# One token group's second dense product as seven block products, with its sums in the activation buffer and the output weights loaded in row order

## The chip, the cores and the metric

The kernel runs on one core of one Trainium2 chip. The metric is the device time of one execution in microseconds (us). Lower is better. Five engines work in parallel, each on a queue of its own, in order: PE (TensorE, matrix products out of SBUF into PSUM), DVE (VectorE), ACT (ScalarE), POOL (GpSimd) and SP (SyncE, which issues nearly all DMAs). They wait for one another by semaphores.

## The reference

Two layers follow each other. The first is a linear attention with decay, for 4 batches, 8 heads, 768 positions and 64 channels a head; a matrix `kv_state` per head is carried from block to block:

```python
Dmask = np.where(rel >= 0, lam[:, None, None] ** rel[None, :, :], 0.0)
for b in range(nb):                    # 12 blocks of 64 positions
    intra = np.einsum('bhic,bhjc->bhij', qb, kb) * Dmask[None]
    intra = np.einsum('bhij,bhjd->bhid', intra, vb)
    inter = np.einsum('bhid,bhde->bhie', qb * lam_pow[None], kv_state)
    out[:, :, sl] = intra + inter
    kb_dec = kb * rev_pow[None]
    kv_state = lam_block * kv_state + np.einsum('bhsd,bhse->bhde', kb_dec, vb)
```

Its result, 4 x 768 = 3072 tokens of 512 channels, goes through a two-layer network of 2048 hidden units:

```python
h = x @ w_in                           # (3072, 512) @ (512, 2048)
g = 0.5 * h * (1.0 + np.tanh(c * (h + 0.044715 * h * h * h)))
return g @ w_out                       # (3072, 2048) @ (2048, 512), float32
```

Everything comes in and goes out as float32; on the chip the products are made in float16 with float32 sums.

## The kernel before, in words

**Two streams of work, one order.** The attention is cut into 24 steps: a step is 256 positions of one batch and half of the heads, so steps 0 and 1 make the first 256 tokens, 2 and 3 the next. The network is cut into seven groups of tokens, `groups = [[0, 1], [2], [3], [4, 5], [6, 7], [8, 9], [10, 11]]`, in units of 256 tokens: group 0 and groups 3 to 6 have 512 tokens, groups 1 and 2 have 256. A group can begin when its steps are done. `queue_group` (L544) cuts a group into small pieces and appends them to the list `filler`; `fill(n)` takes the next n pieces off it. The main sequence (from L922) is a list written out by hand: steps of the attention and `fill` calls in turn. Every instruction is pinned to the program's order (`pin`), so each engine's queue holds its instructions just as the main sequence gives them. Nothing is reordered: where an engine waits for an operand, all that stands behind waits too.

**One attention step.** `load_step` (L60) issues the loads of q, k and v on SP. `cast_q` (L277) multiplies q by its decay on DVE, `cast_k` (L290) makes k float16 (ACT; for step 4 DVE), `scale_v` (L264) multiplies v by its decay on POOL. `prep` makes the three. Four buffers are held for each of the loaded q, k, v, so the load of step s + 4 waits for the use of step s. `stage_t` (L309) transposes q and k on PE into one PSUM tile `Tps` and copies it out (`qkT`); from step 8 on a transposing DMA does this. `R(n, s)` makes the scores S of step n (L350), the products of step s, and the masked scores PT (L360, DVE, from PSUM). `update` (L491) folds the step into the state `t` (L506, DVE) and multiplies the state by the decay into `u` (L513, POOL), which later products read. `U(n)` is the second half of that.

**One group of the network.** `mm1` (L561) makes a tile of the hidden layer, four matmuls deep, and ACT applies GELU to it into `gT` (L565). `gtp` holds two `gT` buffers, so that one group's second product can run while the next group's first is made. `gT` is 16 chunks of 128 hidden units, by all tokens of the group; HF = 8 chunks are one half.

The second product is made in two ways:

- group 0 densely: `mm2(tau, part)` (L570) multiplies tile tau of 128 tokens (0 to 3) by four chunks of hidden units, four matmuls of 128x512 into one bank of PSUM. 4 tiles x 4 parts = 16 pieces, 64 matmuls. A finished tile is copied by ACT into `o32` and sent by `store_pair` (L539), two tiles at a time, from two places in the main sequence;
- groups 1 to 6 by seven products of half size (the Strassen-Winograd scheme). The 2048 hidden units and the 512 outputs and the tokens are halved, so `gT` and `w_out` are each four blocks. `sum_g` (L602) makes four sums of blocks of `gT` on DVE (L610), `sum_wout` (L122) four sums of blocks of `w_out` (L133, DVE), once for all groups, into `w_sum16`. `product(m, p, part)` (L616) then makes product m of 1 to 7 for token tile p, as matmuls of 256 columns (L640): eight, or four where `part` says which half of the hidden units. Results are put together from banks X (a running sum of products 1, 6, 7, 4, read out on the way), W (2) and Y (5, then 3 on top of it), with copies on ACT (L657) and three additions (DVE twice, POOL once, L692). `FACTORS` gives for each product which block or sum of `gT` meets which block or sum of `w_out`: products 1 and 2 need plain blocks, 5 needs sum 1 of both, 6 sum 2, 3 sum 4 of `gT`, 7 sum 3 of both, and 4 sum 4 of `w_out`. Groups 5 and 6 (`SEVEN`) have their first product in seven blocks as well.

The sums of `gT` need a place. `gs_tiles` (L522) gives groups 1 and 2 the staging buffers of the weights, `w0` and `w1`, that are idle by then.

**Output weights.** `load_wout(j)` (L96) loads rows 512 j to 512 j + 511 of `w_out`, 1 MB, into a staging buffer; the order is j = 0, 2, 1, 3. `cast_wout(j, eng)` (L112) makes them float16, in two halves on two engines: j = 0 both on POOL, 2 both on ACT, 1 and 3 one on POOL and one on ACT. A sum `sum_wout(0, m)` needs blocks 0 and 2, `sum_wout(1, m)` blocks 1 and 3.

**The order before.** In the main sequence (L977 to L1013) stand, in this order: 8 pieces (the last of group 0's hidden layer), the casts of `w_out`, five of the eight weight sums, 9 pieces of the dense product, `prep(4)`, `stage_t(4)`, and then steps 5 to 7, each with its `prep`, `R`, `U`, two pieces, and now and then a weight sum. The last piece of the dense product stands just after `U(6)`; behind it begins the hidden layer of group 1.

Of the kernel before, what the change touches and what calls it, by code (L numbers as in the profile page):

```python
# [15 lines left out]
def kernel(  # L16
# [79 lines left out]
    def load_wout(j):  # L96
        t = wst.tile([P, 4, DM], FP32, tag=f"w{(0, 2, 1, 3)[j]}", name=f"wo32_{j}")
        pin(nc.sync.dma_start(out=t[:], in_=moe_w_out[j * 512 : (j + 1) * 512, :].rearrange(
            "(c p) e -> p c e", p=P)))
        wstage[("o", j)] = t  # L100
# [11 lines left out]
    def cast_wout(j, eng):  # L112
        t = wstage[("o", j)]
        for i in range(2):
            dst = w_out16[:, 4 * j + 2 * i : 4 * j + 2 * i + 2, :]
            src = t[:, 2 * i : 2 * i + 2, :]
            if eng[i] is nc.scalar:
                pin(nc.scalar.activation(out=dst, in_=src, func=AF.Copy))
            else:
                pin(nc.gpsimd.tensor_copy(out=dst, in_=src))  # L120
# [44 lines left out]
    for j in (0, 2, 1, 3):  # L165
        load_wout(j)
# [78 lines left out]
    def prep(s):  # L245
        prep_qk(s)
        prep_v(s)
# [42 lines left out]
    def cast_k(s):  # L290
        tk, k32 = a16[s][1], ld32[s][1]
        if s == 4:
            pin(nc.vector.tensor_copy(out=wide(tk), in_=k32[:]))
        else:
            pin(nc.scalar.activation(out=wide(tk), in_=k32[:], func=AF.Copy))  # L295
# [226 lines left out]
    def gs_tiles(g):  # L522
        if g < 3:
# [13 lines left out]
    o_pairs = {}  # L537

    def store_pair(pair):  # L539
        rows = out[2 * pair * P : 2 * pair * P + 2 * P, :].rearrange("(i p) d -> p i d", p=P)  # L540
        for i in range(2):
            pin(nc.sync.dma_start(out=rows[:, i], in_=o_pairs[pair][:, i]))

    def queue_group(g, lead=0, per_set=0):  # L544
# [23 lines left out]
        O2 = {}  # L568

        def mm2(tau, part):  # L570

            if not O2.get(tau):
                O2[tau] = [ps_M.tile([P, DM], FP32, tag="M", name="O2ps"), 0]
            for f in range(4 * part, 4 * part + 4):
                n = O2[tau][1]
                pin(nc.tensor.matmul(O2[tau][0][:], gT[:, f % HF, f // HF, tau * P : (tau + 1) * P],  # L576
                                     w_out16[:, f, :], start=(n == 0), stop=(n == NF - 1)))
                O2[tau][1] += 1
            if O2[tau][1] < NF:
                return  # L580
            pair = tau // 2
            if pair not in o_pairs:
                o_pairs[pair] = otp.tile([P, 2, DM], FP32, tag="o32", name="o32")
            pin(nc.scalar.activation(out=o_pairs[pair][:, tau % 2], in_=O2.pop(tau)[0][:],
                                     func=AF.Copy))

# [27 lines left out]
        def product(m, p, part=None):  # L616
# [42 lines left out]
            def store(T, ps=slice(0, NP), es=slice(0, 2)):  # L659
# [8 lines left out]
                if g == 2:  # L668
                    kept_stores.append(send)
                else:  # L670
                    send()
# [166 lines left out]
        if g == 0:  # L838
# [9 lines left out]
            order = [(tau, part) for part in (0, 2, 1, 3) for tau in range(3)]  # L848
            order += [(3, part) for part in (0, 2, 1, 3)]
            for tau, part in order:  # L850
                filler.append(lambda tau=tau, part=part: mm2(tau, part))
# [127 lines left out]
    fill(8)  # L979
    cast_wout(2, (ACT, ACT))  # L980
    cast_wout(1, (POOL, ACT))
    cast_wout(3, (POOL, ACT))
    for m in W_SUMS:
        sum_wout(0, m, DVE)
    sum_wout(1, 1, DVE)
    fill(9)
    prep(4)
    stage_t(4)
    prep(5)
    sum_wout(1, 2, DVE)  # L990
    fill(2)
# [3 lines left out]
    prep(6)  # L995
    fill(2)
# [4 lines left out]
    sum_wout(1, 3, DVE)  # L1001
# [3 lines left out]
    fill(1)  # L1005
# [3 lines left out]
    sum_wout(1, 4, DVE)  # L1009
    fill(2)  # L1010
    R(7, 6, lambda: prep_qk(9))
    store_pair(0)
# [5 lines left out]
    for n, (a, b, c, d) in FILL.items():  # L1018
# [11 lines left out]
        if n == 9:  # L1030
            store_pair(1)
# [121 lines left out]
```

## Time and profile before

| what | value |
| --- | --- |
| median of 3 runs | 199.15 us (198.92 to 199.36) |
| span of the profiled execution | 197.1 us |
| time of the shown runs beyond that span | 2.05 us |
| busy share of PE, PE's weight loads, DVE, ACT, POOL | 97%, 71%, 77%, 62%, 37% |
| granted clock of PE | 9 tenths or more in every slice of 40 |
| dense second product of group 0 on PE (L576) | from 31.23 to 49.28, with attention steps in between |
| mean DMA rate over the span | 193 GB/s (38.13 MB in both directions) |

The profile is that of one execution, 197.1 us from first to last instruction; a run's time is what the device counts around it, so the two are compared by their difference. The page cuts the span in 40 slices of 4.93 us and gives for each engine its busy tenths (9 is 90% or more). Rows by line give the tile written, the tile read, shapes, how often, and the mean length of one. In the chain of waits, each step leads back from the last instruction to what released it. Lines of the order of time give start, length, engine, line, operation, tiles, and in brackets the idle time before the instruction, with what ended it.

### The profile page before, as it was taken

How to read it: one execution, taken by the hardware profiler on the slowest of the kernel's cores; microseconds unless marked ns; L12 is line 12 of the kernel's file. 1: busy time of each engine (PE TensorE's matmuls, PEld its weight loads, DVE VectorE, ACT ScalarE, POOL GpSimd, SP SyncE). 2: the span in 40 equal slices, each digit the busy share in tenths (PEclk: the TensorE clock that was granted, in tenths of full speed). 3: DMA queues.
4: the chain of work that ended last, by engine and by line, in shares of the span. 5: the costliest groups of instructions: out<-in, count | busy, mean ns of one | idle time of the engine just before them, and what ended most of it. 6: DMA issues, size and time to landing. Idle time of an engine off the chain costs nothing.

```text
span 197.1 us, 5915 instructions
## 1 busy us (share of the span) xinstructions
PE 191.5 (97%) x2431; PEld 140.0 (71%) x2431; DVE 151.6 (77%) x297; ACT 122.2 (62%) x249; POOL 73.3 (37%) x85
## 2 busy tenths in 40 slices
PE   8979999999999999999999999999999999999993
PEld 2556544446888888654688764588888888888882
DVE  4797622789999889849999937998668996588620
ACT  3673878357874685686835378844768845779221
POOL 6594123456554841068854517165002030002000
PEclk9999999999999999999999999999999999999999
DMA  6999999999999999999997998400220300030205
GB/s 172 290 324 384 387 387 388 299 287 292 236 216 225 259 343 220 213 266 247 271 268 149 268 328 213 88 4 0 53 85 25 109 6 0 0 110 0 106 19 197
DMA packets 62810, 38.13 MB, mean 193 GB/s; under 512 B 18624, under 2 KB 55744, under 8 KB 62784
## 3 DMA queue, kind: packets, MB, share of 16 engines
q1 hardware_dynamic: 62240, 37.50, 75.0%
q8 instruction: 19, 0.31, 0.6%
q10 hardware_dynamic: 544, 0.26, 0.5%
q14 instruction: 7, 0.06, 0.1%
HBM read 27.26 MB, written 6.29 MB: 170 GB/s over the span
## 4 chain that ended last, share of the span: by engine, by line
PE 89%; SPq 4%; DMA 4%; ACT 0%; issue 0%
PE Hps L561 25%; PE MX L640 18%; PE MY L640 9%; PE HX L739 7%; PE O2ps L576 7%; PE MW L640 4%; DMA wi<-in_moe_w_in_dram 4%; SPq L70 4%; PE HY L739 4%; PE S L350 3%; PE Hps L830 3%; PE HW L739 2%; PE OK L408 2%; PE O L461 1%; PE O L436 1%; PE OK L399 1%
## 5 line engine op out<-in xcount | busy, mean ns | idle before, releaser
L561 PE MATMUL Hps<-xT,w_in 128*128 128x512 f16 (+1 forms) x288 | 50.5, 332 | 0.0
L513 POOL TENSOR_TENSOR u<-t,lumask 128x256 f16<-128x256 f32 x40 | 30.9, 787 | 39.5 <-DVE t L506 25.8
L561 PEld LDWEIGHTS <-w_in 128*128 128x128 f16 x288 | 27.9, 98 | 19.1
L565 ACT ACTIVATE gT<-Hps 128x512 f16<-128x512 f32 x56 | 33.3, 597 | 11.3 <-PE Hps L561 10.8
L360 DVE TENSOR_TENSOR PT<-S,mask 128x512 f16<-128x512 f32 x48 | 30.3, 681 | 7.5 <-PE S L350 7.5
L266 POOL TENSOR_TENSOR v<-v,dv 128x512 f16<-128x512 f32 x24 | 27.7, 1156 | 18.2 <-DMA v<-in_v_dram 14.2
L640 PEld LDWEIGHTS <-gs 128*128 128x128 f16 x320 | 31.2, 98 | 3.6
L640 PEld LDWEIGHTS <-gT 128*128 128x128 f16 x240 | 23.3, 98 | 3.2 <-ACT gT L565 0.2
L640 PE MATMUL MX<-w_sum,gs 128*128 128x256 f16 x160 | 21.4, 273 | 0.0
L282 DVE TENSOR_TENSOR qk<-q,dq 128x512 f16<-128x512 f32 x23 | 18.4, 802 | 1.7 <-DMA q<-in_q_dram 1.7
L692 POOL TENSOR_TENSOR o<-u,q 128x512 f32<-128x512 f32 (+1 forms) x5 | 6.3, 1253 | 35.2 <-ACT u L657 35.2
L295 ACT ACTIVATE qk<-k 128x512 f16<-128x512 f32 x23 | 14.4, 625 | 7.4 <-DMA k<-in_k_dram 7.2
L610 DVE TENSOR_TENSOR gs<-gT 128x1024 f16<-128x1024 f16 (+1 forms) x24 | 16.9, 711 | 1.6 <-ACT gT L565 1.6
L576 PE MATMUL O2ps<-w_out,gT 128*128 128x512 f16 x64 | 14.6, 379 | 0.0
L487 ACT ACTIVATE xT<-OK 128x256 f16<-128x256 f32 x26 | 9.9, 452 | 6.7 <-PE OK L408 6.2
L739 PEld LDWEIGHTS <-ws 128*128 128x128 f16 x128 | 12.5, 97 | 1.8
L657 ACT ACTIVATE u<-MX 128x256 f32<-128x256 f32 x18 | 6.9, 384 | 10.1 <-PE MX L640 10.1
L487 ACT ACTIVATE xT<-O 128x256 f16<-128x256 f32 x22 | 8.0, 459 | 5.3 <-PE O L461 4.5
L576 PEld LDWEIGHTS <-gT 128*128 128x128 f16 x64 | 6.1, 98 | 6.6
L640 PE MATMUL MY<-w_out,gs 128*128 128x256 f16 x80 | 10.7, 273 | 0.0
L350 PEld LDWEIGHTS <-qkT 64*64 64x64 f16 x384 | 6.0, 106 | 6.6 <-issue 3.6
L640 PE MATMUL MX<-w_sum,gT 128*128 128x256 f16 x80 | 10.4, 273 | 0.0
(96 smaller groups left out, 317.3 us busy)
## 6 DMA issues: line engine op xcount, KB each, us to landing
q<-in_q_dram SPq DMA_DIRECT2D x24, 256.0 KB, 5.1
k<-in_k_dram SPq DMA_DIRECT2D x24, 256.0 KB, 5.1
v<-in_v_dram SPq DMA_DIRECT2D x23, 256.0 KB, 5.4
out_dram<-o SPq DMA_DIRECT2D x23, 256.0 KB, 4.2
wo<-in_moe_w_out_dram SPq DMA_DIRECT2D x4, 1024.0 KB, 9.5
wi<-in_moe_w_in_dram SPq DMA_DIRECT2D x4, 512.0 KB, 8.0
wi<-in_moe_w_in_dram SPq DMA_DIRECT2D x2, 1024.0 KB, 12.7
v<-in_v_dram ACTq DMA_DIRECT2D x1, 256.0 KB, 4.2
```

The costliest lines, as they stand in the source:

```text
L266: pin(nc.gpsimd.tensor_tensor(wide(tv[:]), ld32[s][2][:], decay(dv, s), ALU.mult))
L282: pin(q_eng.tensor_tensor(wide(tq), q32[:], decay(dq, s), ALU.mult))
L295: pin(nc.scalar.activation(out=wide(tk), in_=k32[:], func=AF.Copy))
L360: pin(nc.vector.tensor_tensor(t[:, hl].rearrange("p b c d -> p b (c d)"), Sps[:].rearrange("p b c d -> p b (c d)"), mask[:].unsqueeze(1).t ...
L487: pin(nc.scalar.activation(out=d, in_=o, func=AF.Copy))
L513: pin(nc.gpsimd.tensor_tensor(u[:], state[half][:].unsqueeze(2).to_broadcast([P, 2, 2, D]), lumask[:, 2 * half : 2 * half + 2, :].unsqueez ...
L561: pin(nc.tensor.matmul(by_block(Hps[:, i, :]), w_in16[:, c, f * P : (f + 1) * P], x(c), start=(c == 0), stop=(c == NC - 1)))
L565: pin(nc.scalar.activation(out=dst, in_=Hps[:], func=AF.Gelu_apprx_tanh))
L576: pin(nc.tensor.matmul(O2[tau][0][:], gT[:, f % HF, f // HF, tau * P : (tau + 1) * P], w_out16[:, f, :], start=(n == 0), stop=(n == NF - 1)))
L610: pin(nc.vector.tensor_tensor(g_rows(m, i), g_rows(a, i), g_rows(b, i), op))
L640: pin(nc.tensor.matmul(dst, lhsT, rhs, start=(opens and i == 0), stop=(closes and i == HF - 1), skip_group_check=True))
L739: pin(nc.tensor.matmul(dst[:, i, :], w_in_block(a, slice(c, c + 1), slice(f * P, f * P + P))[:, 0], x_block(b, slice(c, c + 1))[:, 0], sta ...
```

## The change

Group 0's second product goes through `product` as the other groups' does. Its pieces stand in the order (1, 0) (5, 0) (1, 1) (5, 1) (2, 0) (3, 0) (6, 0) (2, 1) (6, 1) (3, 1) (7, 0) (7, 1) (4, 0) (4, 1) of (product, half of the hidden units), each for two token tiles: 28 pieces of four matmuls with 256 columns in place of 16 pieces of four with 512. The `mm2` of before is gone.

The eight sums of `gT` for group 0 are made on DVE, each over four chunks and 256 tokens (128x1024). They are held in a second tile of `gtp`, the buffer that group 1's `gT` takes later.

`w_out` is loaded in the order 0, 1, 2, 3. The first half of blocks 1 to 3 is made float16 on DVE, the second on ACT; block 0 stays on POOL. The k of step 4 is made float16 on ACT. The casts and the sums of weights stand at other places between the pieces. Groups of pieces (`fill`) between the attention steps are larger: 4 instead of 2 ahead of `R(4, None)`, for example. The stores of the two halves of group 0's output are kept (`o_sends`) and issued at the places where `store_pair` stood, one row block of 128 tokens a DMA, as before.

```diff
--- before.py
+++ after.py
@@ -94,7 +94,7 @@
         pin(nc.sync.dma_start(out=t[:, cs, :], in_=src[:, cs, :]))
 
     def load_wout(j):
-        t = wst.tile([P, 4, DM], FP32, tag=f"w{(0, 2, 1, 3)[j]}", name=f"wo32_{j}")
+        t = wst.tile([P, 4, DM], FP32, tag=f"w{j}", name=f"wo32_{j}")
         pin(nc.sync.dma_start(out=t[:], in_=moe_w_out[j * 512 : (j + 1) * 512, :].rearrange(
             "(c p) e -> p c e", p=P)))
         wstage[("o", j)] = t
@@ -117,7 +117,7 @@
             if eng[i] is nc.scalar:
                 pin(nc.scalar.activation(out=dst, in_=src, func=AF.Copy))
             else:
-                pin(nc.gpsimd.tensor_copy(out=dst, in_=src))
+                pin(eng[i].tensor_copy(out=dst, in_=src))
 
     def sum_wout(j, m, eng):
 
@@ -162,7 +162,7 @@
     for j in range(1, 4):
         for part in ((0, 1) if j < 2 else (None,)):
             load_win(j, part)
-    for j in (0, 2, 1, 3):
+    for j in range(4):
         load_wout(j)
     for s in range(4, 9):
         load_step(s)
@@ -289,10 +289,7 @@
 
     def cast_k(s):
         tk, k32 = a16[s][1], ld32[s][1]
-        if s == 4:
-            pin(nc.vector.tensor_copy(out=wide(tk), in_=k32[:]))
-        else:
-            pin(nc.scalar.activation(out=wide(tk), in_=k32[:], func=AF.Copy))
+        pin(nc.scalar.activation(out=wide(tk), in_=k32[:], func=AF.Copy))
 
     whole_qk = {}
 
@@ -520,7 +517,13 @@
     gs_kept = []
 
     def gs_tiles(g):
-        if g < 3:
+        if g == 0:
+            if not gs_kept:
+                t = gtp.tile([P, HF, 2, 2 * SB], FP16, tag="gT", name="gs_0")
+                t = t[:].rearrange("p i f n -> p (i f n)").rearrange(
+                    "p (k i n) -> p k i n", k=4, i=HF)
+                gs_kept[:] = [0, t[:, 0:2], t[:, 2:4]]
+        elif g < 3:
             if not gs_kept or gs_kept[0] != g:
                 gs_kept[:] = [g, wst.tile([P, 4, HF, P], FP16, tag=f"w{g - 1}", name=f"gs_{g}")]
         elif not gs_kept or gs_kept[0] < 3:
@@ -534,12 +537,8 @@
     group_of = {sb: (g, i) for g, sbs in enumerate(groups) for i, sb in enumerate(sbs)}
     filler = []
     kept_stores = []
-    o_pairs = {}
-
-    def store_pair(pair):
-        rows = out[2 * pair * P : 2 * pair * P + 2 * P, :].rearrange("(i p) d -> p i d", p=P)
-        for i in range(2):
-            pin(nc.sync.dma_start(out=rows[:, i], in_=o_pairs[pair][:, i]))
+    o_sends = []
+    sum_of = {}
 
     def queue_group(g, lead=0, per_set=0):
         N = len(groups[g]) * SB
@@ -565,27 +564,6 @@
             pin(nc.scalar.activation(out=dst, in_=Hps[:], func=AF.Gelu_apprx_tanh))
 
         row0 = groups[g][0] * SB
-        O2 = {}
-
-        def mm2(tau, part):
-
-            if not O2.get(tau):
-                O2[tau] = [ps_M.tile([P, DM], FP32, tag="M", name="O2ps"), 0]
-            for f in range(4 * part, 4 * part + 4):
-                n = O2[tau][1]
-                pin(nc.tensor.matmul(O2[tau][0][:], gT[:, f % HF, f // HF, tau * P : (tau + 1) * P],
-                                     w_out16[:, f, :], start=(n == 0), stop=(n == NF - 1)))
-                O2[tau][1] += 1
-            if O2[tau][1] < NF:
-                return
-            pair = tau // 2
-            if pair not in o_pairs:
-                o_pairs[pair] = otp.tile([P, 2, DM], FP32, tag="o32", name="o32")
-            pin(nc.scalar.activation(out=o_pairs[pair][:, tau % 2], in_=O2.pop(tau)[0][:],
-                                     func=AF.Copy))
-
-
-
         HN = N // 2
         G_SUMS = {1: ((1, 0), ALU.add, (1, 1)), 2: (1, ALU.subtract, (0, 0)),
                   3: ((0, 0), ALU.subtract, (1, 0)), 4: ((0, 1), ALU.subtract, 2)}
@@ -665,7 +643,9 @@
                     for i in [slice(i, i + 1) for i in range(ps.start, ps.stop)]:
                         pin(nc.sync.dma_start(out=rows[:, i, es], in_=o[:, i, es, :]))
 
-                if g == 2:
+                if g == 0:
+                    o_sends.append(send)
+                elif g == 2:
                     kept_stores.append(send)
                 else:
                     send()
@@ -845,10 +825,11 @@
                     filler.append(lambda f=f, stage=stage: mm1_part(f, *stage))
             for f in range(8, NF):
                 filler.append(lambda f=f: mm1([f]))
-            order = [(tau, part) for part in (0, 2, 1, 3) for tau in range(3)]
-            order += [(3, part) for part in (0, 2, 1, 3)]
-            for tau, part in order:
-                filler.append(lambda tau=tau, part=part: mm2(tau, part))
+            sum_of[0] = sum_g
+            for m, part in ((1, 0), (5, 0), (1, 1), (5, 1), (2, 0), (3, 0), (6, 0), (2, 1), (6, 1),
+                            (3, 1), (7, 0), (7, 1), (4, 0), (4, 1)):
+                for p in range(HN // P):
+                    filler.append(lambda m=m, p=p, part=part: product(m, p, part))
             return
         def behind(k, i0, i1, ms):
 
@@ -976,40 +957,53 @@
     cast_win(3)
     DVE, ACT, POOL = nc.vector, nc.scalar, nc.gpsimd
     cast_wout(0, (POOL, POOL))
-    fill(8)
-    cast_wout(2, (ACT, ACT))
-    cast_wout(1, (POOL, ACT))
-    cast_wout(3, (POOL, ACT))
-    for m in W_SUMS:
-        sum_wout(0, m, DVE)
+    sum_0 = sum_of[0]
+    fill(4)
+    sum_0(0, 4, (1, 2))
+    sum_wout(0, 1, DVE)
+    sum_0(0, 4, (4,))
+    fill(4)
+    cast_wout(1, (DVE, ACT))
+    sum_0(4, 8, (1,))
     sum_wout(1, 1, DVE)
-    fill(9)
+    sum_0(4, 8, (2, 4))
+    fill(6)
+    cast_wout(2, (DVE, ACT))
+    fill(2)
+    sum_wout(0, 2, DVE)
+    sum_wout(0, 3, DVE)
+    sum_0(0, 4, (3,))
+    fill(6)
+    cast_wout(3, (DVE, ACT))
+    sum_wout(1, 2, DVE)
     prep(4)
+    fill(4)
+    sum_0(4, 8, (3,))
     stage_t(4)
     prep(5)
-    sum_wout(1, 2, DVE)
-    fill(2)
+    sum_wout(1, 3, DVE)
+    fill(4)
     R(4, None)
     stage_t(5)
     U(4)
     prep(6)
+    sum_wout(0, 4, DVE)
     fill(2)
     R(5, 4)
     stage_t(6)
     U(5)
     prep(7)
-    sum_wout(1, 3, DVE)
+    sum_wout(1, 4, DVE)
     fill(2)
     R(6, 5)
     U(6)
-    fill(1)
+    fill(2)
     prep(8)
     fill(1)
     stage_t(7)
-    sum_wout(1, 4, DVE)
     fill(2)
     R(7, 6, lambda: prep_qk(9))
-    store_pair(0)
+    o_sends.pop(0)()
     U(7)
     scale_v(9)
     fill(2)
@@ -1028,7 +1022,7 @@
         if n < 11:
             load_step(n + 4, "qkv" if n < 10 else "qk")
         if n == 9:
-            store_pair(1)
+            o_sends.pop(0)()
         if n == 11:
             scale_v(13)
             load_step(14, "v")
```

## The prediction

> **What bounds the kernel now.** I read the busy rows and slices of the page first, then the chain of waits, then the order of time of DVE and of POOL around the change. The page's rows for the whole span:
>
> ```profile
> PE 191.5 (97%) x2431; PEld 140.0 (71%) x2431; DVE 151.6 (77%) x297; ACT 122.2 (62%) x249; POOL 73.3 (37%) x85
> ...
> PE   8979999999999999999999999999999999999993
> ...
> DVE  4797622789999889849999937998668996588620
> ```
>
> PE is the bound: from slice 4 (20 us) almost to the end it has no idle tenth. DVE has a hole in slices 5 to 8 (25 to 40 us, tenths 6, 2, 2, 7), just ahead of the stage that is changed, and from slice 9 on it is nearly full too. The chain of waits has the changed stage; columns are start, length, what:
>
> ```profile
> 24.32 6.91 PE Hps L561 x32
> 31.23 7.77 PE O2ps L576 x36
> 39.00 0.53 PE Tps L321 x8
> 39.53 1.73 PE O2ps L576 x8
> ...
> 48.42 0.86 PE O2ps L576 x4
> 49.28 0.87 PE Hps L561 x8
> ...
> 59.52 0.87 PE MW L640 x8
> ```
>
> The dense product starts at 31.23 and has its last piece done at 49.28, with no gap between pieces. 8 of its 512-column matmuls take 1.73 us, 0.216 each; 8 of the 256-column matmuls of the seven-block form (L640) take 0.87, 0.109 each. Now DVE and POOL in the same stretch (start, length, instruction, idle before it):
>
> ```profile
> 25.90 1.29 DVE L110 CAST w_in<-wi 128x1024 f16<-128x1024 f32 x2 [1.39 <-DMA wi<-in_moe_w_in_dram]
> 30.63 0.69 DVE L133 TENSOR_TENSOR w_sum<-w_out 128x1024 f16<-128x1024 f16 x1 [3.44 <-POOL w_out L120]
> 33.79 0.69 DVE L133 TENSOR_TENSOR w_sum<-w_out,w_sum 128x1024 f16<-128x1024 f16 x1 [2.46 <-ACT w_out L118]
> 34.40 1.52 DVE L133 TENSOR_TENSOR w_sum<-w_out 128x1024 f16<-128x1024 f16 x1
> ...
> 46.78 1.10 DVE L133 TENSOR_TENSOR w_sum<-w_out 128x1024 f16<-128x1024 f16 x1
> ```
>
> ```profile
> 28.58 2.02 POOL L120 CAST w_out<-wo 128x1024 f16<-128x1024 f32 x2 [6.56 <-DMA wo<-in_moe_w_out_dram]
> 33.99 1.38 POOL L120 CAST w_out<-wo 128x1024 f16<-128x1024 f32 x1 [3.40 <-DMA wo<-in_moe_w_out_dram]
> ...
> 46.43 0.90 POOL L513 TENSOR_TENSOR u<-t,lumask 128x256 f16<-128x256 f32 x1 [0.49 <-DVE t L506]
> 47.55 1.22 POOL L266 TENSOR_TENSOR v<-v,dv 128x512 f16<-128x512 f32 x1 [0.22 <-DMA v<-in_v_dram]
> ```
>
> Two things are to be seen. DVE's hole is some 6 us of waiting for output weights. And DVE and POOL take turns: the sum of 0.69 us at 34.40 took 1.52 and ended 0.55 after POOL's cast (33.99 to 35.37); that cast took 1.38 instead of 1.01 because the sum before it ran to 34.48. Likewise the sum at 46.78 ended 0.55 after POOL's u (47.33), and POOL's v at 47.55 ended 0.90 after that sum (47.88). So where a DVE operation reads two SBUF tensors beside a POOL operation, the second waits for the whole of the first. Operations that read PSUM (L360 at 42.32, 0.68 long beside a v of 1.04) don't show it.
>
> **PE's part.** Out go 64 matmuls, 64 x 0.216 = 13.83 us; in come 7 products x 2 tiles x 8 blocks = 112 of 256 columns, 112 x 0.109 = 12.23. On a PE that never waits that is -1.60 us. Weight loads rise from 64 to 112, 98 ns each by the row of L640, under a matmul of 109: covered, as everywhere in L640. The Trainium skill differs here: "TensorE: Matmul & The Clock Gate", Back-to-back issue gap, gives a sustained 81 ns per matmul at 128 columns and 131 ns at 512, with weight loads in the stream. By a straight line between them 256 columns cost about 98 (my estimate), and the sum would be 112 x 98 ns less 64 x 131 ns, 2.6 us more. The chain above decides for 0.216 and 0.109.
>
> **Where the saving falls.** 18 half products (4 matmuls, 0.437 us each) stand ahead of the transposes of step 4, 7.86 us, against 36 dense matmuls, 7.77. Up to there nothing is saved; the 1.6 us lie in the ten pieces behind.
>
> **What DVE gets.** New: 8 sums of gT (L610 form 128x1024), 3 casts of output weights (128x1024), 2 output sums from PSUM (128x512); gone: the k cast of step 4. Back to back each of the new ones costs 0.605 us (35.84 to 36.44; the two casts at 25.90 take 1.29 with their overlap), so 13 x 0.605 - 0.35 = +7.5 us, more than the hole. The eight sums of the weights stay but move ahead. POOL loses two casts and gets one 128x512 sum, about 1.04 us by the v rows of that shape. ACT loses one weight cast and four copies of O2ps (0.58) and gets nine small copies (0.38 to 0.60) and the k cast: I cost it at nothing, since what PE waits for on it (the halves of blocks 1 to 3 at about 32.8, 35.7 and 37.9, from casts of 1.05 us) is never last below.
>
> **DVE's queue, one by one.** It is in order, so a product that needs one tensor waits for all ahead of it. The weights land as now: blocks 0 to 3 of w_out at 28.5, 31.2, 33.9, 36.8 (the casts that wait for them).
> - Sum 1 of gT (first half) starts when ACT's GELU number 12 ends, 28.45, and runs to 29.13. POOL's first cast, ready at 28.58, then takes its turn to 30.03; sum 2 to 30.57; POOL's second cast to 31.47 instead of 30.60. The first weight sum waits for it: 31.51 to 32.19.
> - From there 13 more, one each 0.605 with 0.05 to 0.1 where one needs the one before: sum 4; cast of block 1 (ends 33.40); sum 1; weight sum 1 of the second half (34.61); sums 2 and 4; cast of block 2 (36.53); weight sums 2 and 3; sum 3; cast of block 3 (39.06); weight sum 2, second half (39.78).
> - PE against this: product 1 is up to 0.1 late, 5 another 0.1, 1b waits for 33.40 (0.3), 5b for 34.61 (0.3), and product 2, ready at 35.53, waits until 36.6 for the cast of block 2: 1.1 us. Then PE runs to 41.0 without a wait.
> - POOL's v of step 4, landed at 39.54, gets the turn at 39.78; the q product of step 4 follows it and ends at 41.26 (now 38.56). The transposes of step 4 start at 41.35 instead of 39.00: **+2.35 us**.
> - Behind it: output sum, sum 3, copy of qkT (43.07), q of step 5 after POOL's v (43.95), weight sum 3 (44.55), output sum, the two masks PT of step 4 (46.36), the state (46.74). Now these masks end at 43.00. POOL's u of step 4 needs the state, takes its turn after the q of step 6 (47.34) and ends at 47.81; PE has been at that product since 46.7: 1.2 us. Queued behind u stand v of step 6 (49.27), the output sum on POOL (50.3) and u of step 5, which also lets q of step 7 ahead: 51.3. PE waits for that u from 50.65, 0.8 us; small waits (0.1 to 0.35) are at 7b, S5 and S6.
> - The last weight sum comes after q of step 7 and that u: 51.87. Product 4b waits for it, and the first layer of group 1 starts at about 52.8 instead of 49.28.
>
> **Sum: +3.5 us**, that is, about 5 us of waits on PE less the 1.6 saved. Behind 49.28 PE is full to the end, so nothing gives it back; DVE is 1.28 us lighter there (its weight sum at 51.25 is done), so I see no new wait.
>
> **Bounds.** Below: without any turn-taking, the same queue with 0.605 a piece gives the cast of block 2 at 35.7, the q of step 4 at 39.5, and the last weight sum at 48.8: +0.4 us. Above: the ledger has no cost for restarting PE after some ten waits; 0.05 to 0.1 each (the weight load of 98 ns) gives +4.3. I take the value with turns, as all five rows of this stretch where the two meet show them.
>
> **What is moved but costs nothing.** SyncE's queue keeps its order and its bytes: four loads of w_out of 1 MB, only rows exchanged, and stores of the same rows at the same places. Its loads of steps 8, 9, 10 wait for the q products of 4, 5, 6: 41.3, 44.0, 47.3 against issues at 42.75, 45.56, 48.62, so 1.3 us of cover; if that goes, each load is late by what is missing. The first transposing DMA (50.66, behind the q product of step 8) moves to about 55, its reader S8 from 58.5 to 62.0, and it lands 6.6 us after issue: still ahead.
>
> The profiled execution spans 197.1 us; the median of the three runs is 199.15, 2.05 more, which I hold constant. So 199.15 + 3.5 = 202.6.
>
> **Rivals.**
> - **The ledger with few collisions.** If the phases fall so that DVE and POOL seldom meet, the lower bound is nearer: +0.4 to +2.2, 199.5 to 201.4. For it: a POOL operation just missed costs nothing, and PE's own waits shift what POOL waits for. Against: DVE has no pause left in which POOL could slip in.
> - **Faster.** DVE keeps up and PE's saving comes through: 199.15 - 1.6 = 197.5. It decides at one place, the cast of block 2 that product 2 waits for: it would have to end before 34.7, when PE gets there, and the last weight sum before 46.8. Eleven operations from 28.45 at 0.605 end at 35.1 even if the wait for POOL were nothing, so DVE would have to be faster per piece than any row of these shapes. Were it so, the transposing DMA for S16 would still cap it: issued at 88.73 and landing 4.4 us later at the earliest, 93.1, while S16 starts at about 93.9; 0.8 us of gain, 198.35.
> - **The same.** DVE's waits and PE's saving cancel within 0.4 us (0.2%, about what a measurement of this kernel can tell from no change).
>
> **Chances.** The full ledger 0.57, with its own range 201.4 to 203.6; few collisions 0.28; faster 0.10; the same 0.05. The range 199.5 to 203.7 leaves out the faster and same cases and a little above. Faster by over 0.2%: 0.10; within: 0.06 (with the edge of the second case); slower: 0.84.
>
> **What would show it.** Right: DVE in slices 6 to 9 at nine tenths, PE with gaps ahead of the W product (the block-2 cast), of the transposes of step 4 and of the products with u; POOL's first two casts ending near 31.5; the first Hps of 128x256 at 52 to 53. Wrong: PE without gaps from 31 to 47, or DVE's sums beside POOL's casts at 0.68. The forecast fails if DVE's pieces are closer than 0.6 us, or if the turns fall otherwise.

## The result and the profile after

The changed kernel took 203.87 us (median of 4 runs, 203.46 to 204.44) beside 199.10 for the kernel before: a ratio of 1.0242 with a 95% interval of 1.0223 to 1.0262, so 4.8 us slower. The forecast was 202.6, with a range of 199.5 to 203.7. The direction was right; the size fell out of the range by 0.17 us. Two disturbed executions of the run without sums are left out below (201.75 and 201.87 stay), and the reordered kernel's profile, with a granted clock of 0.89 from 10 to 16 us and of 0.74 from 16 to 20, begins the changed stage 1.1 us late.

The profiled execution spans 202.7 us and is that of the slowest run (204.44). The rows that answer to those shown of before, first the busy rows of the page:

```profile
PE 190.9 (94%) x2477; PEld 144.2 (71%) x2479; DVE 163.0 (80%) x309; ACT 123.4 (61%) x254; POOL 74.1 (37%) x84
...
PE   8879999897799999999799999999999999999993
...
DVE  4987568999999979879989937999778997588620
```

PE has less work than before (190.9 us against 191.5) in a longer span. Behind slice 2 (slices are counted from 0) its tenths fall below 9 in slices 7, 9 and 10 (35 to 40 us and 46 to 56 us) and once more in slice 19 (96 to 101 us). DVE has lost its hole: slice 6 is at 8, and slices 7 to 13 are at nine tenths or more. The chain of waits (start, length, what) now runs through DVE in the stage that was changed:

```profile
31.43 0.69 DVE w_sum L133
32.12 0.60 DVE gs L588
...
38.46 0.62 DVE w_out L120
39.17 0.69 DVE w_sum L133
39.86 1.45 DVE qk L282
...
51.04 1.03 DVE w_sum L133
52.11 1.03 PE MX L618 x8
53.14 0.87 PE Hps L560 x8
...
63.38 0.87 PE MW L618 x8
...
92.47 6.66 DMA qkT<-qk
99.17 0.42 PE S L347 x16
```

The first hidden layer of group 1 starts at 53.14 instead of 49.28, 3.86 us later. The second place is at the end of the lines: the scores of step 16 hang on a transposing DMA, which was not in the chain before. PE's waits from 28 us on (us in total, times, the longest) name both:

```profile
PE OK L405 <- POOL u L510: 1.6, 2, 0.8
PE S L347 <- DMA qkT<-qk: 1.3, 1, 1.3
PE MW L618 <- DVE w_out L120: 0.9, 1, 0.9
PE S L347 <- ACT qkT L325: 0.6, 2, 0.3
PE Tps L318 <- DVE qk L282: 0.3, 1, 0.3
```

The kernel before has not one line in this view. In the order of time of DVE and of POOL, the turns are where they were expected:

```profile
29.09 1.41 DVE L588 TENSOR_TENSOR gs<-gs,gT 128x1024 f16<-128x1024 f16 x1
31.43 0.69 DVE L133 TENSOR_TENSOR w_sum<-w_out 128x1024 f16<-128x1024 f16 x1 [0.94 <-POOL w_out L120]
...
39.78 1.53 DVE L282 TENSOR_TENSOR qk<-q,dq 128x512 f16<-128x512 f32 x1
```

```profile
28.59 2.80 POOL L120 CAST w_out<-wo 128x1024 f16<-128x1024 f32 x2 [6.66 <-DMA wo<-in_moe_w_out_dram]
39.52 1.24 POOL L266 TENSOR_TENSOR v<-v,dv 128x512 f16<-128x512 f32 x1 [8.13 <-DMA v<-in_v_dram]
```

Sum 2 took 1.41 us beside a cast on POOL, against 0.69 alone. The q product of step 4 took 1.53 behind v. It ended at 41.31, and the transposes of step 4 could not start before that.

To compare runs, the stage is cut in two by three rows of the order of time: the start of group 0's second product, of the transposes of step 4, and of group 1's hidden layer. "Excess" is what is lost behind that: how much later than in the kernel before the hidden-layer pieces behind the scores of step 16 begin (95.37 in its chain), less how much later group 1's hidden layer begins (49.28 there). Times are medians, each taken beside the kernel before at 198.93 to 199.10; the other columns come from one profiled execution each.

| kernel | time, us | product to step 4 | step 4 to group 1 | sum | excess up to step 16 |
| --- | --- | --- | --- | --- | --- |
| before | 199.10 | 7.77 | 10.28 | 18.05 | |
| changed | 203.87 | 10.39 | 11.61 | 22.00 | 1.49 |
| e1, no sums of gT | 201.75, 201.87 | 8.81 | 10.97 | 19.78 | 0.88 |
| e2, casts on ACT | 204.77 | 10.47 | 11.61 | 22.08 | 0.65 |
| e3, block 0 on DVE | 203.26 | 9.25 | 12.09 | 21.34 | 0.65 |
| e4, DMA of step 16 early | 203.44 | 10.37 | 11.62 | 21.99 | 0.17 |
| f1, late weight sums moved too | 202.27 | 8.45 | 9.79 | 18.24 | 2.66 |
| f2, output sum late | 203.31 | 10.39 | 11.11 | 21.50 | 0.37 |
| f4, reordered | 202.05 | 8.48 | 11.63 | 20.11 | 0.00 |
| g1, dense with DVE's work | 201.47 | 10.39 | 10.13 | 20.52 | 0.00 |
| g2, more cover | 204.89 | 10.39 | 11.94 | 22.33 | 1.25 |
| g4, casts on POOL | 204.71 | 10.76 | 11.62 | 22.38 | 0.54 |

### The profile page after: what moved, and what is told of

Same layout as the page of the kernel before. It is cut to its first block, busy times and chain, and to the rows that moved or that the text cites. A ratio compares the mean times of both kernels' runs of the same rounds, so it can differ in the third digit from the quotient of the medians.

```text
span 202.7 us, 6031 instructions
## 1 busy us (share of the span) xinstructions
PE 190.9 (94%) x2477; PEld 144.2 (71%) x2479; DVE 163.0 (80%) x309; ACT 123.4 (61%) x254; POOL 74.1 (37%) x84
## 4 chain that ended last, share of the span: by engine, by line
PE 69%; DMA 12%; DVE 10%; SPq 4%; POOL 1%; issue 1%; ACT 1%; DVEq 0%
PE Hps L560 18%; PE MX L618 18%; PE MY L618 9%; PE HX L719 7%; DMA wo<-in_moe_w_out_dram 5%; PE MW L618 4%; DMA wi<-in_moe_w_in_dram 4%; SPq L70 4%; PE HY L719 4%; DMA qkT<-qk 3%; DVE w_sum L133 3%; PE S L347 3%; DVE qk L282 2%; PE HW L719 2%; DVE gs L588 2%; POOL w_out L120 1%
## 5 line engine op out<-in xcount | busy, mean ns | idle before, releaser
L560 PE MATMUL Hps<-xT,w_in 128*128 128x512 f16 (+1 forms) x288 | 50.5, 332 | 0.0
L618 PEld LDWEIGHTS <-gs 128*128 128x128 f16 x384 | 37.3, 98 | 4.8 <-issue 0.3
L618 PEld LDWEIGHTS <-gT 128*128 128x128 f16 x288 | 27.8, 98 | 6.0 <-DVE w_out L120 1.2
L618 PE MATMUL MX<-w_sum,gs 128*128 128x256 f16 x192 | 25.5, 273 | 0.0
L588 DVE TENSOR_TENSOR gs<-gT 128x1024 f16<-128x1024 f16 (+1 forms) x28 | 20.3, 731 | 3.6 <-ACT gT L564 3.6
L282 DVE TENSOR_TENSOR qk<-q,dq 128x512 f16<-128x512 f32 x23 | 21.5, 937 | 0.0
L618 PE MATMUL MY<-w_out,gs 128*128 128x256 f16 x96 | 12.8, 273 | 0.0
L618 PE MATMUL MX<-w_sum,gT 128*128 128x256 f16 x96 | 12.4, 273 | 0.3 <-DVE w_sum L133 0.3
L618 PE MATMUL MW<-w_out,gT 128*128 128x256 f16 x96 | 11.8, 273 | 0.9 <-DVE w_out L120 0.9
L618 PE MATMUL MY<-w_sum,gs 128*128 128x256 f16 x96 | 12.3, 273 | 0.2 <-DVE w_sum L133 0.2
L618 PE MATMUL MX<-w_out,gT 128*128 128x256 f16 x96 | 12.0, 273 | 0.2 <-DVE w_out L120 0.2
```

The lines of the kernel that those rows point to most:

```text
L282: pin(q_eng.tensor_tensor(wide(tq), q32[:], decay(dq, s), ALU.mult))
L560: pin(nc.tensor.matmul(by_block(Hps[:, i, :]), w_in16[:, c, f * P : (f + 1) * P], x(c), start=(c == 0), stop=(c == NC - 1)))
L588: pin(nc.vector.tensor_tensor(g_rows(m, i), g_rows(a, i), g_rows(b, i), op))
L618: pin(nc.tensor.matmul(dst, lhsT, rhs, start=(opens and i == 0), stop=(closes and i == HF - 1), skip_group_check=True))
```

## The experiments

The theory: VectorE's in-order queue, with its turns against GpSimd, sets the time from 28 to 52 us. Its rivals: the seven-block form costs PE the time by itself; the load order does; the halved cover between the attention steps does (ahead of the scores of steps 5 and 6 still stand two pieces, but a piece is now 0.44 us of PE's work instead of 0.86; only ahead of those of step 4 did the number double); and for the part behind 53 us, the transposing DMA of step 16.

### VectorE's part alone, with the dense product (g1)

```diff
-            for m, part in ((1, 0), (5, 0), (1, 1), ...): ... product(m, p, part)
+            order = [(tau, part) for part in range(4) for tau in range(3)]
+            order += [(3, part) for part in range(4)]
+            for tau, part in order:
+                filler.append(lambda tau=tau, part=part: mm2(tau, part))
...
-    fill(6)
+    fill(3)
```

> The changed kernel with the dense second product of group 0 put back (16 pieces, parts in the order 0 to 3, 9 of them ahead of step 4 and 2, 2, 2, 1 between the steps as before), while VectorE's casts, sums of weights and the eight sums of gT stay where the change put them; the sums of gT are read by nobody. Theory (VectorE's queue sets the time, in whatever form the product is): the q product of step 4 still ends at about 41.2 and its transposes start at about 41.3, 2.3 us later than before; from there PE's 10.28 us of the kernel before give 51.6 to 52.2 for the first hidden layer of group 1, so 2.3 to 2.9 us more, and with 0 to 1 us at the transposing DMA of step 16 the time is 201.4 to 203.0. Rival (the seven-block form itself costs the time, by its waits for sums and its short pieces): no wait ahead of step 4, and within 0.8 us of the kernel before, at most 199.8.

It took 201.47 us, a ratio of 1.0147 (1.0107 to 1.0188). Chain and PE's waits of this kernel:

```profile
39.81 1.46 DVE qk L282
41.32 0.62 PE Tps L318 x8
...
51.61 0.87 PE Hps L566 x8
```

```profile
PE Tps L318 <- DVE qk L282: 2.1, 1, 2.1
PE O2ps L581 <- DVE w_out L120: 0.2, 1, 0.2
```

The dense product waits for no sum, and still the transposes of step 4 start at 41.32, as in the changed kernel, since the q product of step 4 stands behind the same 13 operations from 31.4 us on. That is one wait of 2.1 us in one place, 2.5 us in the time: half of the loss, with PE's form of product taken out, and as the theory had it (201.4 to 203.0; the rival gave at most 199.8). From there to group 1 it needs 10.13 us, no more than before, so the late casts and sums hurt there only where a product waits for them. The changed kernel needs 11.61, although PE's own work is less by 1.68: seven dense pieces (6.05 us) have become ten half pieces (4.37).

### Without the sums of gT (e1), and without the late weight sums too (f1)

```diff
+            if t in G_SUMS and g:
+                return gsum[t][:, i, :]
             if t in G_SUMS:
-                return gsum[t][:, i, :]
+                t = ((1, 0), (0, 0), (0, 1), (1, 1))[t - 1]
...
-            for m in ms:
+            for m in (ms if g else ()):
```

> The changed kernel without the eight sums of gT of group 0: products 5, 6, 3 and 7 read a plain block of gT in place of a sum, so group 0's output is wrong, while PE, ACT, POOL and the loads do the same as before. Theory (VectorE's queue is the bound from 28 to 52 us): eight operations of 0.605 us, 4.8 us, leave it; PE's waits for casts, q and u go, PE keeps its saving of 1.6, and the first hidden layer of group 1 starts at about 47.8 instead of 53.14. Then 197.5 to 198.5, the upper end where the transposing DMA of step 16 comes last. Rival (the smaller matmuls, their restarts or the load order cost PE the time, whatever VectorE does): still above 202.

Both kernels leave out group 0's sums of gT, so its output is not the product. In f1, group 0's products read plain blocks of the output weights as well, and the three late weight sums move:

```diff
-    sum_wout(1, 3, DVE)
     fill(4)
     R(4, None)
...
-    sum_wout(0, 4, DVE)
...
-    sum_wout(1, 4, DVE)
     fill(2)
     R(6, 5)
     U(6)
     fill(2)
+    sum_wout(1, 3, DVE)
+    sum_wout(0, 4, DVE)
+    sum_wout(1, 4, DVE)
     prep(8)
```

> The changed kernel without the sums of gT of group 0, as in the run without sums, and with group 0's products reading plain blocks of the output weights in place of weight sums, so that the three weight sums that stood between attention steps 4 to 7 can be made behind U(6); group 0's output is wrong. Theory (VectorE's own queue sets the pace of steps 4 to 7 even without the sums of gT): the transposes of step 4 start at about 40.0 as without sums, and the stretch from there to the first hidden layer of group 1 shrinks from 10.97 to 8.6 to 9.3 us, so that starts at 48.7 to 49.4; time 198.5 to 200.5, by what the transposing DMA of step 16 adds. Rival (two half pieces of 0.44 us between the attention steps are too short a cover for scores, mask, state and u, whatever else VectorE has to do): the waits for u of 0.8 and for the copies of the transposes stay, and it starts at 50.5 or later.

Both theories missed in e1. Taking 4.8 us off VectorE shortened the stage by 2.2, not by 5.3: 1.6 ahead of step 4 and 0.6 behind. Behind step 4 VectorE is as busy as in the changed kernel, without a gap from 41.19 to 51, because a copy, masks, states, q products, output sums and three weight sums are left. f1 takes the three weight sums out of there, and this part falls to 9.79, the whole stage to 18.24, 0.19 above the kernel before. So the loss of the stage is VectorE's: the sums of gT ahead of step 4, the weight sums behind it. What f1 moved came back at step 7 (order of time of DVE, then of PE, in f1):

```profile
50.44 2.55 DVE L133 TENSOR_TENSOR w_sum<-w_out,w_sum 128x1024 f16<-128x1024 f16 x2
52.91 0.68 DVE L282 TENSOR_TENSOR qk<-q,dq 128x512 f16<-128x512 f32 x1
53.51 0.68 DVE L327 COPY qkT<-Tps 128x1024 f16<-128x1024 f16 x1
```

```profile
54.24 0.42 PE L347 MATMUL S<-qkT 64*64 64x128 f16 x16 [1.61 <-DVE qkT L327]
```

The scores of step 7 wait 1.61 us for a copy behind those sums, and the scores of step 16 wait 0.6 for their transposing DMA. Most of what f1 took above its expectation (202.27 against 198.5 to 200.5) is these two waits: work on a full queue that is pushed back is not gone. f1 also shows a floor. Even where no product waits for a sum, the 1.6 us that PE saves do not appear. Two waits of 0.30 us for copies of the transposes on ACT and one of 0.36 for u stay in the stage, as f1's rival (the short cover) had it, though it starts group 1 well before the rival's 50.5; how much of the floor they make was not isolated.

### Block casts on other engines (e2, e3, g4)

```diff
-    cast_wout(0, (POOL, POOL))
...
+    cast_wout(0, (DVE, DVE))      # e3, between sums 1 and 2 of gT
...
-    cast_wout(1, (DVE, ACT))
+    cast_wout(1, (ACT, ACT))      # e2; 2 and 3 likewise
+    cast_wout(1, (POOL, ACT))     # g4; 2 and 3 likewise
```

> The changed kernel with the first halves of blocks 1 to 3 of the output weights cast on ScalarE too, so VectorE loses three casts of 0.605 us. Theory (VectorE's queue): product 2 no longer waits 0.9 us for the cast of block 2, and everything behind is up to 1.8 us earlier: first hidden layer of group 1 at 51.3 to 51.6, time 201.9 to 202.4. Rival (the weights themselves land too late in row order): the wait ahead of product 2 stays, with another releaser, and the time stays within 0.4 us of 203.9.

> The changed kernel with both casts of block 0 on VectorE, between sums 1 and 2 of gT, instead of on GpSimd. VectorE has 1.2 us more work, and nobody to take turns with from 28 to 39 us. Theory (taking turns costs as much as the work): sum 2 no longer takes 1.41 us, the first weight sum no longer waits 0.94 us for GpSimd; the work from there on is 0 to 0.5 us earlier, time 203.3 to 203.9. Rival (only the amount of VectorE's own work counts): 1.2 us more, 204.8 to 205.2.

> The changed kernel with the first halves of blocks 1 to 3 cast on GpSimd again, as in the kernel before. Theory (GpSimd and VectorE take turns): each cast of about 1.0 us on GpSimd holds VectorE up for that long, against 0.605 for VectorE doing it itself, and product 2 waits no less; 0 to 1.4 us slower than the changed kernel, 203.8 to 205.3. Rival (only VectorE's own work counts): 1.8 us of work leave VectorE, 202.0 to 202.7.

e2 came out at 204.77, outside both ranges. Product 2 still waits about 1.0 us, with another releaser, as the rival had it, but the cause is not late weights. The chain of waits in e2 shows ACT's own order:

```profile
33.89 0.83 PE MX L618 x6
34.74 0.38 ACT m L635
35.13 1.89 ACT w_out L118 x2
37.02 0.49 ACT q L635
37.51 1.90 ACT w_out L118 x2
39.42 0.69 DVE w_sum L133
```

The casts of block 2 stand behind the copy of product 1, which waits for product 1, which waits for the casts of block 1. One full queue was exchanged for another: the last cast ends at 39.41 where VectorE ended it at 39.08. This is why nothing was gained; the profiled execution took 203.93, and what the others (up to 205.28) lost beyond it is not shown.

e3 gave 203.26, 0.04 below the range of the theory of turns and far from its rival's: VectorE does 1.2 us more, and the stretch up to step 4 is 1.14 us shorter. 0.48 of that is given back behind step 4. g4 gave 204.71, as the same theory had it; a weight sum of g4 beside POOL's third cast, from the order of time of DVE and POOL:

```profile
31.34 1.54 DVE L133 TENSOR_TENSOR w_sum<-w_out 128x1024 f16<-128x1024 f16 x1 [0.93 <-POOL w_out L120]
```

```profile
28.59 3.75 POOL L120 CAST w_out<-wo 128x1024 f16<-128x1024 f32 x3 [6.75 <-DMA wo<-in_moe_w_out_dram]
```

The same sum took 0.69 in the changed kernel, where POOL was idle by then. The Trainium skill, "SBUF — State Buffer", section "SBUF: two separate sides", says that an operation of VectorE with two SBUF inputs and one of GpSimd that reads SBUF contend for a shared pair of ports: whichever starts first has it for its whole instruction, and the other is blocked; the 1.54 against 0.69 here and the 1.41 above agree with it.

### Cover between the steps, and GpSimd's output sum (g2, f2)

```diff
     prep(4)
-    fill(4)
...
-    fill(2)      # g2: two of them, ahead of R(5, 4) and of R(6, 5)
+    fill(4)
```

> The changed kernel with four half pieces more between the steps: 14 instead of 18 ahead of the transposes of step 4, then 4, 4, 4 and 2 instead of 4, 2, 2 and 2. Theory (VectorE is busy without a pause from 31.4 to 52 us, so PE only waits elsewhere): VectorE still has no idle time between steps 4 and 7, its last weight sum ends at 51.5 to 52.2, the first hidden layer of group 1 starts at 52.5 to 53.3, time 203.2 to 204.0. Rival (the halved cover between the steps): the waits for u go without others in their place, and it starts 1 us or more earlier, time 202.0 to 202.9.

```diff
-                    pin(nc.gpsimd.tensor_tensor(out_tile(1)[:, :, 1, :], ...))
+                    late.append(add)      # f2: called behind U(6)
```

> The changed kernel with GpSimd's output sum of group 0 (1.27 us, ahead of u of step 5) moved behind U(6). Theory (VectorE is the bound): the wait of 0.81 us for u of step 5 shrinks or goes, but the last weight sum still ends at about 52 us and product 4 waits for it; time 0 to 0.3 us less, 203.5 to 203.9. Rival (GpSimd's queue ahead of u is the bound): 0.8 less, about 203.0.

g2 took 204.89. The waits for u are gone, as the rival had it, and others stand in their place: 2.1 us for the q product of step 4 instead of 0.3, and 1.4 for a copy of product 7 on ACT. Its hidden layer of group 1 starts at 53.67, 0.4 past what either theory gave. The last weight sum ended at 52.02, within the theory's range, and VectorE has no pause above 0.15 us between step 4 and that sum. But the wait of 1.4 is not VectorE's: in g2's chain it hangs on ACT's queue, where copies into xT and qkT and a k cast stand ahead of the copy of product 7. Four half pieces, 1.75 us of PE's work, went behind step 4; the first part stayed at 10.39 and the second grew by 0.33. So cover moved from the one side to the other gains nothing here; that the short cover has no part in the loss is not shown.

f2 took 203.31, between the two expectations. The wait for u of step 5 fell from 0.81 to about 0.3, and the second part is 0.5 us shorter. The theory had missed that the q product of step 7, which took 1.10 behind that u, would then take 0.60 on VectorE itself. So some of VectorE's time is GpSimd's doing.

### The order of loading alone (g3), and a reordered VectorE queue (f4)

```diff
-    for j in (0, 2, 1, 3):
+    for j in range(4):
...
-            order = [(tau, part) for part in (0, 2, 1, 3) for tau in range(3)]
+            order = [(tau, part) for part in range(4) for tau in range(3)]
...
-    cast_wout(2, (ACT, ACT))
-    cast_wout(1, (POOL, ACT))
+    cast_wout(1, (ACT, ACT))
+    cast_wout(2, (POOL, ACT))
```

> The kernel before with only the order of the output weights changed: rows loaded in the order 0, 1, 2, 3, the dense pieces in the same order of parts, casts on ScalarE and GpSimd as before in that order, the weight sums of the second half first. Theory (the load order is no cause): block 2 is float16 at about 35 us and its first dense piece starts at 36.4, so nothing waits, and the time is 198.8 to 199.3. Rival (row order makes PE wait for weights): 0.5 us or more above.

It took 198.94, a ratio of 0.9998 (0.9989 to 1.0008). The load order costs the dense kernel nothing.

```diff
-    cast_wout(0, (POOL, POOL))
...
-    sum_0(0, 4, (1, 2))
+    sum_0(0, 4, (1,))
+    cast_wout(0, (DVE, DVE))
     sum_wout(0, 1, DVE)
-    sum_0(0, 4, (4,))
+    sum_0(0, 4, (2,))
...
-    sum_0(4, 8, (2, 4))
-    fill(6)
+    sum_0(0, 4, (4,))
+    fill(4)
     cast_wout(2, (DVE, ACT))
-    fill(2)
+    sum_0(4, 8, (2,))
     sum_wout(0, 2, DVE)
+    fill(4)
+    sum_0(4, 8, (4,))
     sum_wout(0, 3, DVE)
...
-        elif s in (5, 6, 8):
+        elif s in (4, 5, 6, 8):
```

> The changed kernel with VectorE's queue ordered by when the weights land: casts of block 0 on VectorE, each block's cast and weight sum as soon as it can be, sums of gT in between, the copy of the transposes of step 4 on ScalarE, GpSimd's output sum behind U(6), the transposing DMA of step 16 early. Theory (the loss is VectorE's order and load, not the product form): about 3 us come back; product 2 starts at 35.0 to 35.5 instead of 36.52, the transposes of step 4 at 39.5 to 40.0, the first hidden layer of group 1 at 50.0 to 50.8; time 199.5 to 200.6. Rival (halved cover between the steps): it starts at 51.5 or later, time above 201.3.

The order by landing times, with f2's and e4's edits in it, took 202.05 (200.63 to 202.34). The part up to step 4 fell to 8.48, 1.91 of the 2.62 us back. The part behind stayed at 11.63: the copy of step 4's transposes had left VectorE and GpSimd's output sum had left the way, but one sum of gT had come in, beside v. Without the late start of its profiled execution, the transposes of step 4 stand at 39.5 and group 1 at 51.3, so the expectation held in the first half and not in the second. The time lies above its range (199.5 to 200.6) and on the side of its rival, the halved cover, which gave more than 201.3. No version of the seven-block form that was tried beats the kernel before.

### The transposing DMA of step 16 (e4, f3, h1, h2)

```diff
             load_step(15, "v")
-            load_step(16, "v")
             scale_v(15)
...
     cast_qk(16)
-    load_step(17, "qk")
     transpose_dma(16)
+    load_step(16, "v")
+    load_step(17, "qk")
     load_step(17, "v")
```

> The changed kernel with the transposing DMA of step 16 issued ahead of the loads of v 16, q 17 and k 17 on SyncE instead of behind them. Theory (of the loss of 4.8 us, 3.86 lie ahead of group 1 and the rest in the scores of step 16, which wait for that DMA): the DMA is issued some 1.7 us earlier, the scores of step 16 wait no more, the first hidden layer of group 1 stays at 53.1, and the time falls by 0.6 to 1.2 to about 203.0. Rival (the scores of step 16 are not where the rest goes, and the wait returns at the next transposing DMA): within 0.3 us of 203.9.

> The kernel before with the transposing DMA of step 16 issued ahead of the loads of v 16, q 17 and k 17. Theory: nobody waits for that DMA before the change (it lands 0.8 us ahead of its reader), so the time stays within 0.2 us of the kernel before, 199.0. Rival (the loads pushed back are needed, or the DMA was a hidden wait there too): over 0.4 us either way.

The same edit on both kernels gave 203.44 (from 203.38 to 204.85) and 199.23. In the changed kernel the wait at the scores of step 16 was gone in the profile, the excess 0.17 instead of 1.49, but the median fell by only 0.43, less than expected, and the ratio to the kernel before did not fall at all (1.0244, 1.0205 to 1.0284): e4 alone does not price this wait. On the kernel before the edit changed the time by a factor of 1.0012 (1.0003 to 1.0022), 0.26 us where 0.2 was expected, and not for the better, so nothing waits for this DMA there. To settle it, the DMA was taken out of both kernels:

```diff
-        if s >= FIRST_DMA_T:
+        if s >= FIRST_DMA_T and s != 16:
...
-    fill(5)
+    fill(2)
+    stage_t(16)
+    fill(3)
```

> The changed kernel with step 16 transposed on TensorE, as steps 4 to 7 are, in place of the transposing DMA: eight transposes of 0.45 us in all, two pieces of hidden layer after U(14), and a copy on ScalarE. Theory (of the 4.8 us lost, 3.86 lie ahead of group 1's hidden layer and some 0.9 in the scores of step 16, which wait for the transposing DMA): the scores of step 16 wait for no DMA, and the difference to the kernel before with the same edit is 3.6 to 4.2 us; by itself some 0.9 less and 0.45 more than the changed kernel, 203.2 to 203.7. Rival (the 0.9 us are lost elsewhere behind group 1's start, or come back at the next transposing DMA): the difference stays at 4.5 to 5.0.

> The kernel before with step 16 transposed on TensorE at the same place. Theory (that DMA is hidden in the kernel before): only the transposes' 0.45 us are added, 199.3 to 199.7. Rival (a hidden wait there too): no change or faster.

203.43 (ratio 1.0220, 1.0193 to 1.0248) and 199.61 (1.0032, 1.0018 to 1.0046): both as the theory gave them, and 3.82 us apart, where the two kernels with the DMA are 4.77 apart. 3.82 is the shift of group 1's hidden layer (3.86). So some 0.9 us of the loss in the median is this DMA, and the rest is the stage ahead of group 1. The intervals of the two ratios make 3.82 uncertain by about 0.6, and with that of the changed kernel the 0.9 by about 0.7.

## Why the prediction was right, and where it was not

**DVE's queue, one by one: right, within 0.2 us.** Product 2 was to wait until 36.6 and started at 36.52. The transposes of step 4 were to start at 41.35 and did at 41.37. POOL's u of step 4 was to end at 47.81; PE's product with it started at 47.87. The last weight sum was to end at 51.87 and did at 52.06. PE's two waits for u were forecast at 1.2 and 0.8 and are listed at 0.82 and 0.81. Group 1's hidden layer was to start at 52.8 and started at 53.14, 0.34 later. The shift of 3.5 us measured 3.86. The rest of that 0.36 lies within the prediction's own upper bound of 4.3, made of restarts. Run g1 shows the first 2.35 us alone (2.5 in its time). e1 and f1 show that most of the remainder is VectorE too: in f1 the whole stage is 0.19 us above the kernel before.

**Turns between DVE and POOL: right.** The lower bound without turns (+0.4) is contradicted by e3 and g4, which move casts between the two: with more work on VectorE and none on GpSimd the stage is shorter (21.34 against 22.00), with less on VectorE and more on GpSimd longer (22.38). The medians lie the same way, though their intervals overlap that of the changed kernel.

**PE's part: right in price, and worth nothing.** Eight matmuls of 256 columns take 0.87 us in the chain of the changed kernel, as assumed. The other sum, by the Trainium skill's "TensorE: Matmul & The Clock Gate", Back-to-back issue gap, would make it 98 ns for one (the estimate in the prediction); the row here says 109, and the measurement decides. f1 shows that the 1.6 us saved would not have come through even without the sums: its stage is 0.19 us longer than the dense one. What limits it there was isolated by no run.

**The step that failed: "Behind 49.28 PE is full to the end ... so I see no new wait".** PE was not full to the end. The prediction had the transposing DMA of step 16 in hand, with its 0.8 us of cover, but used it only as a cap on a gain, in the rival "Faster". It took for granted that a later stage moves as a whole. The order of time of SP and of PE, in the kernel before and then in the changed one:

```profile
88.73 1.40 SPq L303 DMA_TRANSPOSE qkT<-qk  x1
93.60 0.64 PE L350 MATMUL S<-qkT 64*64 64x128 f16 x32
```

```profile
92.47 2.51 SPq L300 DMA_TRANSPOSE qkT<-qk  x1
99.17 0.42 PE L347 MATMUL S<-qkT 64*64 64x128 f16 x16 [1.29 <-DMA qkT<-qk]
```

The DMA was issued 3.74 us later than before (92.47 against 88.73), about as late as PE, but needed 6.66 us to land instead of 4.36. SP alone was held by it for 1.1 us longer. 0.8 us of cover could not hold 2.3 more. The wait is 1.29 us in the profiled execution (of an excess of 1.49; e4 without the wait keeps 0.17). In the medians it is some 0.9, uncertain by 0.7, and without it the forecast would have been 0.3 to 0.4 us off, inside the range. Why the DMA took longer stays open.

**The span against the time.** The 2.05 us held constant were too many. The changed kernel's runs lie 1.74 to 1.83 us above their spans, and one of before with a span of 197.1 took 198.91; the profiled execution of before was thus one of the quicker ones. It made no difference to the forecast, which used the shift alone.

## What to carry to other kernels

Before moving work onto an engine with a hole in its busy row, write its queue out operation by operation against the landing times and the turns of its neighbours; a hole that is the wait for weights is no room for work that needs the same weights. Ask of every asynchronous transfer behind the change how much cover it has, for losses as for gains: a transfer with less than a microsecond can turn a shift into a shift and a wait. And a saving on the bound engine has to be followed to the next stage's inputs before it is counted.

## What was not expected of the hardware

The same kind of transposing DMA takes very different times: 3.7 us for step 16 in e4, 4.4 in the kernel before, 6.7 in the changed one, 7.2 in e1. In the changed kernel the DMA engines moved almost nothing for 1.4 us in the midst of it. DMA view of the changed kernel, 94 to 99.2 us, in 40 slices of 0.13 us:

```profile
DMA  9878999999999955941999000000000099999999
GB/s 280 248 221 252 291 303 319 309 315 298 402 240 234 154 136 134 116 47 35 205 177 22 0 0 0 2 8 10 10 8 10 12 262 288 330 347 347 185 299 299
...
q8 instruction: 1, 0.02, 2.5%
...
qkT<-qk SPq DMA_TRANSPOSE x1, 6.7
```

And the kernel before, from the issue of that DMA to its landing (88.7 to 93.1):

```profile
DMA  5984678999999999999999995532999999999599
...
qkT<-qk SPq DMA_TRANSPOSE x1, 4.4
```

From 96.7 to 98.2 us the first shows 0 to 22 GB/s; the second never falls below 47. One transfer of instructions lies in the first window and none in the second. Whether that transfer held the others up was not tried.

The wait comes and goes. It is 0.2 to 1.3 us in the profiles of eight changed versions, the changed kernel's own among them (in e2 the view of PE's waits puts it down to another releaser, but the weight loads there wait 0.6 us for this DMA), and there is none of 0.2 or more on PE in the other three that have the DMA, e4, f4 and g1. In those eight, the DMA holds SP for 1.76 to 3.05 us and lands after 6.3 to 7.2; in the three, and in the kernel before, for 1.24 to 1.43 us, and it lands after 3.7 to 5.0. A transfer of instructions on queue q8 lies in the flight of all eight and of none of the three. It is not enough by itself: f3 has one in its flight too and holds SP for 1.87 us, and its DMA landed after 4.1. Nor does an almost empty stretch make the DMA late: e4 and f4 show one of some 0.65 us (6 to 14 GB/s) just behind the issue and land after 3.7, while e3 and f2 show none and land after 6.3. What holds the DMA is not settled by these runs.
